# A DiT block on one core: scores in one block, attention in two halves, and transposes by DMA in place of TensorE

## The chip, the cores and the metric

The kernel runs on one core of a Trainium2 chip. The core has five engines that run side by side, each in the order of its own program: TensorE (PE, matrix multiplication into PSUM), VectorE (DVE), ScalarE (ACT), GpSimd (POOL) and SyncE (SP, which here only issues DMAs). The metric is the device time of one execution in microseconds (us), lower is better.

## The reference

One diffusion-transformer block with B = 2 batches of N = 256 tokens, D = 1152, two heads of width 576, and an MLP of width 4608, in bf16:

```
mod = (silu(c) @ w_mod).reshape(B, 6, 1, D)
shift_a, scale_a, gate_a, shift_m, scale_m, gate_m = [mod[:, i] for i in range(6)]
h = layernorm(x) * (1 + scale_a) + shift_a
q, k, v = split(h @ wqkv)                          # two heads of 576
attn = softmax(q @ k.T * 576 ** -0.5)              # per batch and head, 256 x 256
x = x + gate_a * ((attn @ v) @ wo)
h2 = layernorm(x) * (1 + scale_m) + shift_m
return x + gate_m * (gelu(h2 @ w_fc1) @ w_fc2)
```

## The kernel before

The 512 tokens are four tiles of 128 (`NT` = 4, two per batch). D is nine chunks of 128 (`KD` = 9), numbered 0 to 8. A head is 576 wide, which is four and a half chunks: chunk 4 (`HC`) holds 64 features of head 0 and 64 of head 1 (`HP` = 64). Sections that end in columns go in three panels of 384 (`PW`, `NPD` = 3).

The stages follow one another on PE: K projection with the first layer norm (to 33.5 us in the profile), Q projection (L454), attention scores and V projection interleaved (L482, L506), transposes of the attention weights (L546), attention times values (L567), output projection (`wo_group`, L634), FC1 (L681) and FC2 (L748).

Scores (`score_tile`, L473): one tile of 128 queries by 256 keys for each batch, head and query tile, eight in all, each ahead of one of the first eight V groups (a V group is one token tile by one panel, nine matmuls of 384 columns, L506). Each score tile has five matmuls. The chunk that both heads share is read from `kT4m`, a copy of K's chunk 4 in which the other head's 64 rows are zero. In the same way `v4m` is a zero-padded copy of V's chunk 4. The softmax of a tile is a maximum on DVE (L487), an exponential on ACT (L491), a reciprocal and a multiplication on DVE (L497, L498).

After V, PE transposes the attention weights in 16 blocks of 128x128 (L546), DVE and ACT copy them out of PSUM, and attention times values is made for both batches, chunk pair by chunk pair (L567), into `aT`.

The output projection runs over token tiles and panels, 12 groups (`wo_group`). After each, DVE multiplies by the gate (L640), POOL adds the residual (L641), and DVE gathers statistics (L646). When a tile is complete, `ln2_normalize` takes the root on ACT (L588), reciprocal and bias on DVE (L589, L591) and normalizes on ACT (L594), for the last tile with the tail of the row on DVE (L596). `ln2_transpose` then transposes the normalized chunks on PE (L605) into PSUM, and scales and shifts them on the way out, on ACT (L610) or DVE (L615), into `hT`. These transposes are dripped between matmuls by `filler`: those of batch 0 between the matmuls of the last three projection groups, those of batch 1 within FC1.

FC1 first runs ten of its 36 output chunks for batch 0 alone and then for batch 1 alone (`MSPLIT` = 10, 256-wide matmuls), and the other 26 for both (512-wide). `gate_m` comes from `dot_section` (L445): 18 products on DVE against `w_gate_mT`, a section of w_mod that the DMA engines transpose while loading it (L534). It then makes a round trip through DRAM (`gate_m_finish`). `gate_a` comes from a small section on PE (`gate_natural`, L414), is copied out by DVE and ACT (L422, L424), written to DRAM by POOL's DMAs (L425) and read back broadcast (L428). `shift_m` and `scale_m` are sections of 36 matmuls each (`vec_section`, L381); four matmuls at a time run in column quarters of the array.

Order is the program's order: at its end the kernel chains each engine's instructions in the order in which they were written (L762 to L772), SP among them. All big loads and DMA transposes are issued by SP. Five buffers of 20.7 KB a partition (the pool `wide`) hold all weights in turn, so a load also waits until the buffer's old content has been used. PSUM has six accumulators (`acc_tile`) and two smaller-use buffers (`aux_tile`). A new accumulator takes the buffer that was released first.

Of the kernel before, what the change touches and what calls it, by code (L numbers as in the profile page):

```python
# [19 lines left out]
def kernel(  # L20
# [88 lines left out]
    def load_section(name, s):  # L109
        w = wide_tile(name)  # L110
        for r in range(0, KD, 3):
            nc.sync.dma_start(w[:, r:r + 3, :], wmod_v[:, r:r + 3, s * D:(s + 1) * D])
        return w
# [9 lines left out]
    w_gate_a = load_section("w_gate_a", S_GATE_A)  # L123
    w_v = load_panels("w_v", wqkv_v, 2 * D)
    w_shift_m = load_section("w_shift_m", S_SHIFT_M)
    w_scale_m = load_section("w_scale_m", S_SCALE_M)
    w_o = load_panels("w_o", wo_v, 0)
    w_f1 = [None] * 4
    w_f1[0] = load_panels("w_f1_0", wfc1_v, 0)
    w_f1[1] = load_panels("w_f1_1", wfc1_v, D)  # L130
# [10 lines left out]
    kT4m = act.tile([P, H, T], BF16, name="kT4m")  # L141
    v4m = act.tile([P, NT, H, P], BF16, name="v4m")
    nc.gpsimd.memset(kT4m[HP:P, 0, :], 0.0)
    nc.gpsimd.memset(kT4m[0:HP, 1, :], 0.0)
    nc.gpsimd.memset(v4m[:, :, 0, HP:P], 0.0)
    nc.gpsimd.memset(v4m[:, :, 1, 0:HP], 0.0)

# [138 lines left out]
    def k_evac(m):  # L288
        if m == HC:
            evac(kT4m[0:HP, 0, :], pk[m][0:HP, :])  # L290
            evac(kT4m[HP:P, 1, :], pk[m][HP:P, :])
        else:
            evac(kT[:, m, :], pk[m][:])
# [157 lines left out]
    for m in range(KD):  # L451
# [7 lines left out]
        if m == 6:  # L459
            gate_a = gate_natural(0, w_gate_a)  # L460


    def head_chunks(h):
        return list(range(HC + 1)) if h == 0 else list(range(HC, KD))

    n_s = B * H * TPB
    soft = act.tile([P, 4 * n_s * N], BF16, name="soft", tag="x1")
    e_all = soft[:, 0:2 * n_s * N].bitcast(FP32).rearrange("p (i n) -> p i n", n=N)
    attn_all = soft[:, 2 * n_s * N:3 * n_s * N].rearrange("p (i n) -> p i n", n=N)
    attnT_all = soft[:, 3 * n_s * N:4 * n_s * N].rearrange("p (i c n) -> p i c n", c=TPB, n=N)  # L470
    attn_tiles = {}

    def score_tile(b, h, qt):  # L473
        chunks = head_chunks(h)
        q0 = b * N + qt * P
        ps_s = acc_tile([P, N], "ps_s")
        for i, cc in enumerate(chunks):
            if cc == HC:
                k_ap = kT4m[:, h, b * N:(b + 1) * N]
            else:  # L480
                k_ap = kT[:, cc, b * N:(b + 1) * N]
            nc.tensor.matmul(  # L482
                ps_s[:], qT[:, cc, q0:q0 + P], k_ap,
                start=(i == 0), stop=(i == len(chunks) - 1),
            )
        negmax = small.tile([P, 1], FP32, name="negmax", tag="negmax")
        nc.vector.reduce_max(negmax[:], ps_s[:], axis=AX.X, negate=True)  # L487
        si = (b * H + h) * TPB + qt
        e_sb = e_all[:, si, :]
        rowsum = small.tile([P, 1], FP32, name="rowsum", tag="rowsum")  # L490
        nc.scalar.activation(e_sb, ps_s[:], ACT.Exp, bias=negmax[:], scale=1.0, accum_out=rowsum[:])  # L491
        attn = attn_all[:, si, :]
        attn_tiles[(b, h, qt)] = attn

        def finish():
            rs = small.tile([P, 1], FP32, name="rs", tag="rs")
            nc.vector.reciprocal(rs[:], rowsum[:])  # L497
            nc.vector.tensor_scalar_mul(attn, e_sb, rs[:])  # L498

        return finish  # L500


    def v_group(pnl, t):
# [7 lines left out]
        c4 = HC * P - pnl * PW  # L511
        if 0 <= c4 and c4 + P <= PW:
            evac(v4m[:, t, 0, 0:HP], pacc[:, c4:c4 + HP])
            evac(v4m[:, t, 1, HP:P], pacc[:, c4 + HP:c4 + P])
# [4 lines left out]
    for i, (pnl, t) in enumerate(v_order):  # L519
        fin = score_tile(*score_order[i]) if i < len(score_order) else None  # L520
        v_group(pnl, t)
        if fin is not None:
            fin()
# [135 lines left out]
    while fill:  # L659
        fill.pop(0)()  # L660
# [142 lines left out]
```

## Time and profile before

| | us |
|---|---|
| median of 8 runs (lowest to highest) | 248.93 (248.54 to 249.13) |
| the profiled execution, its time | 248.76 |
| its span, first to last instruction | 247.0 |
| Q projection ends, scores begin | 52.29 |
| V ends, attention transposes begin | 76.85 |
| output projection begins | 82.28 |
| output projection ends, FC1 begins | 100.83 |
| FC2 begins | 173.13 |

The profiled execution's time is 1.76 us more than its span; the span is what the trace explains. The granted TensorE clock was 1.00 throughout. In the profile's rows a busy PE is modelled to the end of its pipeline, so the length of a piece overlaps the start of the next, and costs are best read from start to start. "Idle before" names how long an engine stood still before an instruction and what released it. Times in tables and timelines count from the start of the span. SP's rows ("SPq") are the issue of a DMA, not its transfer.

### The profile page before, as it was taken

The page shows a single profiled execution, that of the slowest core. Times are in us where ns is not written, and L with a number is a line of the kernel's source. Part 1 is how long each engine was busy: PE and PEld are TensorE (multiplying, and loading weights), DVE is VectorE, ACT ScalarE, POOL GpSimd, SP SyncE. Part 2 cuts the span into 40 slices and gives each one's busy share as a digit, 9 for nine tenths or more (in the row PEclk, how much of TensorE's full clock was granted, in tenths as well). Part 3 has the DMA queues.
Part 4 walks back from the last instruction along what each step waited for, and adds up shares of the span by engine and source line. Part 5 has one row for each costly group of instructions (what it writes and reads, how often), then busy time and mean ns, then how long its engine had stood idle before and what let it go on. Part 6 is the DMA issues. An engine that isn't in the chain of part 4 may idle for free.

```text
span 247.0 us, 4011 instructions
## 1 busy us (share of the span) xinstructions
PE 239.0 (97%) x1709; PEld 144.3 (58%) x1709; DVE 88.3 (36%) x209; ACT 68.3 (28%) x133; POOL 34.3 (14%) x53
## 2 busy tenths in 40 slices
PE   6899999999999999989999999999999999999994
PEld 2585444456657766878844444444666666666674
DVE  2752461335444678720099991000011000000001
ACT  6731341243424424593322233322000000000000
POOL 4000021031000266300000003100011122111111
PEclk9999999999999999999999999999999999999999
DMA  6999999999999999999792007999600000000000
GB/s 232 323 335 362 366 332 372 333 363 394 379 327 328 327 327 326 327 292 241 157 330 87 0 3 212 326 343 326 182 16 16 19 16 16 21 16 16 31 20 16
DMA packets 63837, 52.18 MB, mean 211 GB/s; under 512 B 12091, under 2 KB 58571, under 8 KB 63819
## 3 DMA queue, kind: packets, MB, share of 16 engines
q1 hardware_dynamic: 62928, 50.14, 66.9%
q0 software_dynamic: 864, 1.79, 2.1%
q8 instruction: 13, 0.21, 0.4%
q14 instruction: 5, 0.04, 0.0%
q10 hardware_dynamic: 27, 0.00, 0.0%
HBM read 48.08 MB, written 1.19 MB: 199 GB/s over the span
## 4 chain that ended last, share of the span: by engine, by line
PE 90%; DMA 3%; DVE 2%; ACT 2%; issue 1%; SPq 0%; ACTq 0%; DVEq 0%
PE pacc L748 28%; PE pacc L681 26%; PE pacc L506 7%; PE pacc L454 7%; PE pacc L634 7%; PE pk L265 4%; DMA w_scale_a<-in_w_mod_dram 3%; PE pk L298 2%; PE pa L567 2%; PE ps_s L482 2%; PE pn L381 1%; DVE stats L175 1%; PE pt L605 1%; PE pm L233 1%; PE pt L243 1%
## 5 line engine op out<-in xcount | busy, mean ns | idle before, releaser
L681 PE MATMUL pacc<-hT,w_f 128*128 128x512 bf16 (+1 forms) x414 | 71.1, 333 | 0.0
L748 PE MATMUL pacc<-w_f,gT 128*128 128x384 bf16 (+2 forms) x468 | 70.5, 314 | 0.0
L748 PEld LDWEIGHTS <-gT 128*128 128x128 bf16 x468 | 44.4, 98 | 26.3
L681 PEld LDWEIGHTS <-w_f 128*128 128x128 bf16 x414 | 40.3, 98 | 29.4
L754 DVE TENSOR_TENSOR tmp<-pacc,gate 128x384 f32<-128x384 f32 (+2 forms) x13 | 6.8, 527 | 88.0 <-PE pacc L748 88.0
L445 DVE SCALAR_TENSOR_TENSOR late<-w_gate_mT,late 128x1152 bf16<-128x1152 bf16 x18 | 24.4, 1358 | 12.4 <-DMA w_gate_mT<-in_w_mod_dram 11.9
L725 ACT ACTIVATE gT<-pacc 128x512 bf16<-128x512 f32 x26 | 15.5, 597 | 35.0 <-PE pacc L681 35.0
L756 POOL TENSOR_TENSOR o_sb<-tmp,x 128x384 bf16<-128x384 f32 (+1 forms) x12 | 11.7, 971 | 72.9 <-DVE tmp L754 72.9
L506 PE MATMUL pacc<-w_v,hT 128*128 128x384 bf16 x108 | 19.2, 326 | 0.0
L634 PE MATMUL pacc<-w_o,big 128*128 128x384 bf16 x108 | 18.5, 326 | 0.0
L454 PE MATMUL pacc<-hT,w_q 128*128 128x512 bf16 x81 | 17.8, 379 | 0.0
L641 POOL TENSOR_TENSOR x<-tmp,x_sb 128x384 f32<-128x384 f32 x11 | 10.0, 912 | 33.3 <-issue 27.2
L506 PEld LDWEIGHTS <-hT 128*128 128x128 bf16 x108 | 10.4, 98 | 6.3 <-issue 0.5
L634 PEld LDWEIGHTS <-big 128*128 128x128 bf16 x108 | 10.4, 98 | 6.2
L265 PE MATMUL pk<-big,w_k 128*128 128x256 bf16 (+2 forms) x90 | 13.4, 293 | 0.4 <-ACT big L252 0.4
L454 PEld LDWEIGHTS <-w_q 128*128 128x128 bf16 x81 | 7.9, 98 | 9.6 <-issue 0.3
L265 PEld LDWEIGHTS <-w_k 128*128 128x128 bf16 x90 | 7.5, 97 | 3.4 <-DMA w_k<-in_wqkv_dram 0.3
L436 POOL DMA_DIRECT2D gates_dram<-grow x4 | 2.0, 513 | 45.5 <-DVE grow L711 45.5
L284 DVE TENSOR_SCALAR big<-pacc 128x512 bf16<-128x512 f32 x5 | 3.5, 691 | 13.3 <-PE pacc L454 13.3
L640 DVE TENSOR_TENSOR tmp<-pacc,gate 128x384 f32<-128x384 f32 x12 | 6.7, 556 | 3.7 <-PE pacc L634 3.6
L697 ACT ACTIVATE gT<-pacc 128x512 bf16<-128x512 f32 x10 | 5.9, 598 | 7.4 <-PE pacc L681 7.4
L158 PE MATMUL pwarm<-zeros 128*128 128x512 bf16 x19 | 6.7, 501 | 1.2 <-DVE eps_t L92 1.2
(109 smaller groups left out, 171.3 us busy)
## 6 DMA issues: line engine op xcount, KB each, us to landing
w_f<-in_w_fc_dram SPq DMA_DIRECT2D x14, 864.0 KB, 10.2
w_f<-in_w_fc_dram SPq DMA_DIRECT2D x2, 2592.0 KB, 18.5
w_f<-in_w_fc_dram SPq DMA_DIRECT2D x2, 1728.0 KB, 13.3
w_shift_a<-in_w_mod_dram SPq DMA_DIRECT2D x3, 864.0 KB, 11.0
w_q<-in_wqkv_dram SPq DMA_DIRECT2D x3, 864.0 KB, 12.2
w_gate_a<-in_w_mod_dram SPq DMA_DIRECT2D x3, 864.0 KB, 10.1
w_v<-in_wqkv_dram SPq DMA_DIRECT2D x3, 864.0 KB, 12.7
w_shift_m<-in_w_mod_dram SPq DMA_DIRECT2D x3, 864.0 KB, 10.2
```

The lines of the kernel that those rows point to most:

```text
L158: nc.tensor.matmul(dst[:], zeros[:, 0:P], zeros[:], start=True, stop=True)
L265: nc.tensor.matmul(pk[m][:, c0:c1], w_k[:, k, m * P:(m + 1) * P], hT0[:, k, c0:c1], start=(k == 0 and c0 == 0), stop=(k == KD - 1), skip_g ...
L445: nc.vector.scalar_tensor_tensor(spill, wT[:, j, :], 1.0, s_all[:, b, :], op0=ALU.mult, op1=ALU.mult, accum_out=dst[:, b * KD + j:b * KD + ...
L454: nc.tensor.matmul(pacc[:], w_q[:, k, m * P:(m + 1) * P], hT[:, k, :], start=(k == 0), stop=(k == KD - 1),)
L506: nc.tensor.matmul(pacc[:], hT[:, k, t * P:(t + 1) * P], w_v[:, k, pnl * PW:(pnl + 1) * PW], start=(k == 0), stop=(k == KD - 1),)
L634: nc.tensor.matmul(pacc[:], aT[:, k, t * P:(t + 1) * P], w_o[:, k, c0:c1], start=(k == 0), stop=(k == KD - 1),)
L641: (nc.gpsimd if pool_add else nc.vector).tensor_tensor(x1[:, t, c0:c1], tmp[:], x_sb[:, t, c0:c1], op=ALU.add)
L681: nc.tensor.matmul(dst, w_f1[m // KD][:, k, ml * P:(ml + 1) * P], hT[:, k, c0:c1], start=(k == 0), stop=(k == KD - 1),)
L725: nc.scalar.activation(gT[:, m, :], pacc[:], ACT.Gelu_apprx_tanh)
L748: nc.tensor.matmul(pacc[:], gT[:, kk, t * P:(t + 1) * P], w_f2[j][:, r, c0 - n * PW:c0 - n * PW + cw], start=(kk == 0), stop=(kk == KF - 1),)
L754: nc.vector.tensor_tensor(tmp[:], pacc[:], gate_m[:, b, c0:c0 + cw], op=ALU.mult)
L756: (nc.vector if last else nc.gpsimd).tensor_tensor(o_sb[:], tmp[:], x1[:, t, c0:c0 + cw], op=ALU.add)
```

## The change

- Scores are made in one block ahead of V: for each batch and head one accumulator of 128 x 2 x 256 is filled by four full chunks, then the shared chunk 4 is added by matmuls over 64 rows only, at row position 0 for head 0 and 64 for head 1. `kT4m` and `v4m`, their memsets and their evictions are gone.
- The softmax is made per batch and head (`softmax`): one maximum over both query tiles, two exponentials, one reciprocal, two multiplications. The first two stand ahead of V group 0, the third ahead of group 1, the fourth ahead of group 2.
- The attention weights of a batch are transposed by one DMA from SBUF to SBUF (`attn_transpose`, issued by SP) in place of eight PE transposes and their copies.
- The gate section moves from the Q stage to after V group 1.
- Attention times values and the first half of the output projection are made for batch 0, then attention times values for batch 1, then the `shift_m` and `scale_m` sections (which stood in V), then the second half of the projection. The shared chunk is made for both batches at once from 64-column matmuls (`pv_shared`).
- After the layer norm of a token tile one DMA transposes it from SBUF into `hT` (`ln2_transpose`), and `ln2_modulate` scales and shifts `hT` in place, two of three chunks on DVE, the third on ACT: batch 0 after projection group (3,0), batch 1 after the last matmuls of FC1's batch-0 part. The `filler` is gone.
- `MSPLIT` is 8 in place of 10.
- Loads on SP stand in another order: w_v ahead of w_gate_a; w_o and w_shift_m ahead of the attention transposes; w_scale_m and w_f1_0 behind them; w_f1_1, w_f1_2, w_f1_3 and w_gate_mT behind the last LN2 transpose.
- The residual addition of the last panel of tiles 1 and 3 is DVE's, all others POOL's (before: of tile 3 alone).

```diff
-    w_gate_a = load_section("w_gate_a", S_GATE_A)
+    w_gate_a = wide_tile("w_gate_a")
     w_v = load_panels("w_v", wqkv_v, 2 * D)
+    load_section("w_gate_a", S_GATE_A, w_gate_a)
+    w_o = load_panels("w_o", wo_v, 0)
     w_shift_m = load_section("w_shift_m", S_SHIFT_M)
-    w_scale_m = load_section("w_scale_m", S_SCALE_M)
-    w_o = load_panels("w_o", wo_v, 0)
-    w_f1 = [None] * 4
-    w_f1[0] = load_panels("w_f1_0", wfc1_v, 0)
-    w_f1[1] = load_panels("w_f1_1", wfc1_v, D)
...
+    scores = {}
+    for b in range(B):
+        for h in range(H):
+            scores[b, h] = acc_tile([P, TPB, N], "ps_s")
+            for qt in range(TPB):
+                q0 = b * N + qt * P
+                for i in range(HC):
+                    cc = h * (HC + 1) + i
+                    nc.tensor.matmul(
+                        scores[b, h][:, qt, :], qT[:, cc, q0:q0 + P], kT[:, cc, b * N:(b + 1) * N],
+                        start=(qt == 0 and i == 0), stop=False, skip_group_check=True,
+                    )
+    for b in range(B):
+        for qt in range(TPB):
+            q0 = b * N + qt * P
+            for h in range(H):
+                rows = slice(h * HP, (h + 1) * HP)
+                nc.tensor.matmul(
+                    scores[b, h][:, qt, :], qT[rows, HC, q0:q0 + P], kT[rows, HC, b * N:(b + 1) * N],
+                    start=False, stop=True, skip_group_check=True, tile_position=(h * HP, 0),
+                )
+
+    def softmax(b, h):
+        ps_s = scores[b, h]
+        negmax = small.tile([P, TPB], FP32, name="negmax", tag="negmax")
         nc.vector.reduce_max(negmax[:], ps_s[:], axis=AX.X, negate=True)
+        rowsum = small.tile([P, TPB], FP32, name="rowsum", tag="rowsum")
+        s0 = (b * H + h) * TPB
+        for qt in range(TPB):
+            nc.scalar.activation(
+                e_all[:, s0 + qt, :], ps_s[:, qt, :], ACT.Exp, bias=negmax[:, qt:qt + 1], scale=1.0,
+                accum_out=rowsum[:, qt:qt + 1],
+            )
+        rs = small.tile([P, TPB], FP32, name="rs", tag="rs")
+        nc.vector.reciprocal(rs[:], rowsum[:])
+        for qt in range(TPB):
+            nc.vector.tensor_scalar_mul(attn_all[:, s0 + qt, :], e_all[:, s0 + qt, :], rs[:, qt:qt + 1])
+
+    def attn_transpose(b):
+        n_b = H * TPB
+        nc.sync.dma_start_transpose(
+            attnT_all[:, b, :, :],
+            attn_all[:, b * n_b:(b + 1) * n_b, :].rearrange("p i n -> p (i n)"),
+        )
...
     for i, (pnl, t) in enumerate(v_order):
-        fin = score_tile(*score_order[i]) if i < len(score_order) else None
+        for j in ((0, 1), (2,), (3,))[i] if i < 3 else ():
+            softmax(j // H, j % H)
+            if j % H == H - 1:
+                attn_transpose(j // H)
         v_group(pnl, t)
+        if i == 1:
+            gate_a = gate_natural(0, w_gate_a)
+
+    w_scale_m = load_section("w_scale_m", S_SCALE_M)
+    w_f1 = [None] * 4
+    w_f1[0] = load_panels("w_f1_0", wfc1_v, 0)
...
+    def pv_shared():
+        pa = acc_tile([P, B, TPB, P], "pa")
+        for b in range(B):
+            for kc in range(TPB):
+                for h in range(H):
+                    f0 = HC * P + h * HP
                     nc.tensor.matmul(
+                        pa[h * HP:(h + 1) * HP, b, :, :], v_sb[:, b * TPB + kc, f0:f0 + HP], attnT(b, h, kc),
+                        start=(b == 0 and kc == 0), stop=(kc == TPB - 1),
+                        skip_group_check=True, tile_position=(0, h * HP),
                     )
+        evac(aT[:, HC, :], pa[:].rearrange("p b q n -> p (b q n)"))
+
+    pv_chunks(0, 0)
+    pv_chunks(0, 1)
+    pv_shared()
...
+    def ln2_transpose(t):
+        nc.sync.dma_start_transpose(hT[:, :, t * P:(t + 1) * P], xn2[t][:])
+
+    def ln2_modulate(b):
+        for k in range(KD):
+            h = hT[:, k, b * N:(b + 1) * N]
+            if k % 3 == 2:
                 nc.scalar.activation(
+                    h, h, ACT.Identity, bias=shift_m[:, k, b:b + 1], scale=scale_m[:, k, b:b + 1],
                 )
             else:
                 nc.vector.tensor_scalar(
+                    h, h, scale_m[:, k, b:b + 1], shift_m[:, k, b:b + 1], op0=ALU.mult, op1=ALU.add,
                 )
...
     for o, (t, i) in enumerate(order):
-        if (t, i) == (3, 0):
-            fill_ln2(0, 5)
-        wo_group(t, i, o < len(order) - 1)
-        if o:
+        wo_group(t, i)
+        if o and (t, i) != (TPB, 0):
             ln2_stats(*order[o - 1])
-    while fill:
-        fill.pop(0)()
-    ln2_normalize(NT - 2, False)
+        if (t, i) == (TPB - 1, NPD - 1):
+            ln2_stats(t, i)
+            pv_chunks(1, 0)
+            pv_chunks(1, 1)
+            shift_m = vec_section(sT, w_shift_m, "shift_m")
+            scale_m = vec_section(sT, w_scale_m, "scale_m")
+            nc.vector.tensor_scalar_add(scale_m[:, :, 0:B], scale_m[:, :, 0:B], 1.0)
+        if (t, i) == (NT - 1, 0):
+            ln2_modulate(0)
     ln2_stats(*order[-1])
+
+    w_f1[1] = load_panels("w_f1_1", wfc1_v, D)
+    w_f1[2] = load_panels("w_f1_2", wfc1_v, 2 * D)
+    w_f1[3] = load_panels("w_f1_3", wfc1_v, 3 * D)
+    w_gate_mT = wide_tile("w_gate_mT")
...
-    MSPLIT = 10
+    MSPLIT = 8
...
+            if b == 0 and m0 == MSPLIT - 2:
+                ln2_modulate(1)
             nc.scalar.activation(gT[:, m0:m0 + 2, b * N:(b + 1) * N], pacc[:], ACT.Gelu_apprx_tanh)
```

## The prediction, as it was made before the result was known

> **What bounds the kernel now.** I read the busy shares first, then the slices, then TensorE's timeline over the stage that changes, and last the DMA queue's own issues.
>
> From the page's busy list and slices:
>
> ```profile
> PE 239.0 (97%) x1709; PEld 144.3 (58%) x1709; DVE 88.3 (36%) x209; ACT 68.3 (28%) x133; POOL 34.3 (14%) x53
> ...
> PE   6899999999999999989999999999999999999994
> ...
> DMA  6999999999999999999792007999600000000000
> ```
>
> TensorE (PE) is busy from slice 2 to the end, so a microsecond counts only if it leaves PE's order of work or is put into it. The DMA engines are nearly full up to about 123 us: a transfer put in there stands behind others.
>
> PE's timeline (start, length, line, operation, count, idle before it):
>
> ```profile
> 48.40 4.06 PE L454 MATMUL pacc<-hT,w_q 128*128 128x512 bf16 x18
> ...
> 76.85 1.06 PE L546 MATMUL pTt<-ident,soft 128*128 128x128 bf16 x16
> 77.91 1.03 PE L567 MATMUL pa<-soft,big 128*128 128x256 bf16 x8
> ...
> 96.25 0.39 PE L605 MATMUL pt<-ident,xn 128*128 128x128 bf16 x4
> 96.47 0.98 PE L634 MATMUL pacc<-w_o,big 128*128 128x384 bf16 x5
> ...
> 100.83 5.40 PE L681 MATMUL pacc<-hT,w_f 128*128 128x256 bf16 x48
> ...
> 109.41 0.38 PE L605 MATMUL pt<-ident,xn 128*128 128x128 bf16 x4 [0.98 <-ACT hT L610]
> 109.63 1.04 PE L681 MATMUL pacc<-hT,w_f 128*128 128x256 bf16 x8
> ```
>
> Lengths overlap the next piece by PE's pipeline, so I take costs from start to start: a 128x128 transpose 0.055 us (76.85 to 77.91 is 16 of them; 96.25 to 96.47 is 4), a 256-wide matmul 0.109 (5.24 for 48), a 384-wide one 0.163 (0.81 for 5), a 512-wide one 0.217. The output-projection stage ends at 100.83, FC2 begins at 173.13. The only wait of this stage is the 0.98 us.
>
> SP's queue and who waited for the last of its transposes:
>
> ```profile
> 101.87 9.81 SPq L534 DMA_TRANSPOSE w_gate_mT<-in_w_mod_dram  x1
> 111.73 3.85 SPq L534 DMA_TRANSPOSE w_gate_mT<-in_w_mod_dram  x1
> 115.62 4.09 SPq L534 DMA_TRANSPOSE w_gate_mT<-in_w_mod_dram  x1
> 123.51 1.36 DVE L445 SCALAR_TENSOR_TENSOR late<-w_gate_mT,late 128x1152 bf16<-128x1152 bf16 x1 [11.86 <-DMA w_gate_mT<-in_w_mod_dram]
> ```
>
> These are the trace's only DMA transposes: 27 blocks of 128x128 each. Issuing takes 3.85 to 4.09 us (the first, 9.81, stood behind loads), and the last landed at 123.4, 7.8 us after its issue began.
>
> **The change, part by part.**
>
> *PE work that goes.* 16 attention transposes: 0.89. 36 LN2 transposes: 36 x 0.055 = 1.98. The 0.98 us wait for a transposed PSUM tile goes with its tile. FC1 with the split at 8 in place of 10 costs the same (two 256-wide matmuls 0.218, one 512-wide 0.217). The gate section (1.21, from 47.19 to 48.40) moves from the Q stage into the V stage: nothing on PE. PE sum: -3.85. The four memsets on POOL and the split evictions into kT4m and v4m also go: worth nothing, as the memsets end at 3.2 us, while PE's first real work waits for w_scale_a until 8.8, and the evictions lie under V's matmuls.
>
> *Half-height and half-width matmuls.* The chunk shared by both heads took 8 zero-padded matmuls in the scores and 8 in attention times values, 0.87 each. Now each 8 are half-array ones, in neighbouring pairs that can run together. Nearest row: the four-way packed section at 74.16 takes 1.22 us to its end at 75.38 for 9 slots of four 288-wide matmuls, 1.08 of streaming (288/256 x 0.109 x 9 is 1.10) and some 0.14 extra. So 4 slots x 0.109 + 0.14 = 0.58 each: -0.29 twice, -0.6. Ends: no pairing, 0; pairing free of extras, -0.87. The Trainium skill's page "TensorEngine Tiling (Array Packing)", "Key Properties", says that changing the tiling mode drains the array; the 0.14 is what the row shows of that, and I use it.
>
> *Softmax in one go per batch and head.* The reduction now spans 512 PSUM columns: 0.42 us at 256, plus 0.27 (copies L282 take 0.425 at 256 columns and 0.692 at 512), 0.68. Then two exponentials with accumulator reads (1.02), reciprocal, two multiplications, some 2.6 us for each of four, in series, since VectorE (DVE) waits for ScalarE (ACT) inside each. Q ends at 52.29 - 1.21 = 51.1, scores (32 x 0.109 + 0.58) at 55.15. The first two are done at about 60.2. Behind them on DVE: V's first eviction, the third softmax, the gate's copies, the fourth, done at 66.8. V's fifth group takes the buffer of V's first (evicted at 60.7, wanted at 62.2), the sixth that of the third softmax (62.4 against 63.7), the eighth that of the fourth (65.9 against 66.6). So no wait on PE, by as little as 0.7. The gate's copies start at 63.2 rather than 48.5; from copy to landed gate the old trace takes some 15 us (copies 48.49, second broadcast issued 56.9, landing 6 to 8 later), giving 78.2, and its first reader is due at about 78.2. A late gate delays DVE, and PE has six accumulators ahead of it: nothing.
>
> *Attention transposes on SP.* Issued at 60.3 and 66.9, behind the loads through w_shift_m; what SP has behind them is w_scale_m and w_f1_0, wanted at 88 and 98. Before, the 28th load was issued at 53.27 and landed some 15 us later, at 68 to 69. The two transposes (8 blocks each, 1.2 us at 4.09/27 a block) land behind it at 70 to 72. V ends at 55.15 + 12 x 1.465 + 1.21 = 73.9: hidden, by 2 to 4 us. Without that cover it would be PE time one for one.
>
> *Values of batch 0, projection, batch 1.* 16 x 0.109 + 0.58: to 76.3. The projection reads chunk 4 after four matmuls (0.65), but that is the one evicted last (0.2 latency + 0.69): PE waits 0.3 to 0.7, I take 0.5. Six groups of 9 x 0.163 to 85.6; values of batch 1 1.74; two sections 2.43, moved here from V; six groups: projection ends at 98.5, against 100.83.
>
> *LN2 of batch 0.* Tile 1 follows the old last tile's chain (100.83 to 106.05, less 0.8 for work of another tile in it): normalized at 90.0, transposed by 94. DVE comes to the modulation only after tile 2's statistics, at 97.75: six operations at 0.20 (L402's row: 12 in 2.44). ACT comes to its three only after normalizing tile 2 (1.35, L594). Projection group (3,0) ends at 95.6; with the old spacing tmp to ACT's normalize 2.16, ACT is free at 99.3, and chunk 2 is ready at 99.7, wanted at 98.7. Chunks 5 and 8 follow 0.42 apart. FC1 loses 1.2 us, and its first half runs 72 x 0.109 = 7.85, to 107.6.
>
> *LN2 of batch 1, the term that decides.* After 98.5 DVE still has tmp(3,1), its statistics, tmp(3,2), the addition, two statistics (0.5 each), aggregation, root, reciprocal, bias; ACT's 640 columns end at 104.2. The transpose: 9 blocks from SBUF, with SP and the DMA engines idle. By the row: issue 9/27 x 4 = 1.35, then the tail after issue (123.4 - 119.7 = 3.7, partly its own backlog, so 1.5 to 3.7): 3 to 5, I take 4.0. A rule speaks against it: "VectorE: DVE Perf Modes", "The three transpose paths", gives 1309 ns for one 128x128 block by the DMA crossbar. Nine in a row would be 11.8 us. The row's 27 blocks in 4.1 (0.15 each) say that they overlap, so I follow the row; by the rule the kernel would end 7.8 us later, at 254.7. No trace here shows an SBUF source, which is why it stays in the range. With 4.0: landed 108.2, chunks modulated from 108.6, wanted from 107.6. PE loses 1.1 in all.
>
> *FC1's remaining weights.* w_f1_1 to w_f1_3 now stand on SP behind that last transpose: issued from 105.6, 2.63 us per load. w_f1_1 is wanted at 108.7 + 7.85 + 1.95 = 118.5 and lands by 115; w_f1_2 lands by 123 (wanted 136). The gate's transposed weights follow at 129 and land between 142 and 151; their 25 us of dot products and 16 us of round trip end between 184 and 192. The first reader, at 177, waits, yet PE needs that accumulator only after six groups, at 206. The last w_f2 load waits for those dot products (by 176, landing by 195), wanted at 219. Nothing.
>
> *Sum.* -3.85 - 0.6 + 0.5 + 1.2 + 1.1 = -1.65. Walking the clock gives a little more: 107.6 + 1.1 + 7.85 + 252 x 0.2165 = 171.1 for FC2's start against 173.13, -2.0 (the sum's 0.35 is slack between stages; I keep the clock). Against the profiled 248.76 (span 247.0): 246.8; the shown runs' median, 248.93, gives 246.9. I predict 246.9.
>
> **Rivals.** *No new waits show* (transposes land in 3 us, ACT's queue slips through): -3.85 - 0.6 is 244.5, less up to 0.35 of the slack above: 244.3. For it: both FC1 waits are computed to about 1 us. Against: ACT's order is fixed by the program.
>
> *The batch-1 transpose is slow.* Every microsecond over 4.0 lands on PE. At 6.0 the change is worth nothing; at 8, 250.9; at 11.8, 254.7. For it: an SBUF source is untried here and the crossbar rule. Against: SP and the engines are idle then.
>
> *The attention transposes land after V.* They sit behind a backlog of 8 us and must pass it; from 76 on (2 us late) the gain is gone, at 78 it is 250.9. For it: the first w_gate_mT issue took 9.81 behind loads. Against: 2 to 4 us of cover.
>
> *Halves don't pair up:* +0.6, 247.5, the same side.
>
> **How the numbers follow.** As forecast, 245.6 to 248.2: 0.52. No waits, 243.9 to 245.6: 0.13. A break-even mixture around 248.2 to 249.4: 0.12. Slow batch-1 transpose 0.15 and late attention transposes 0.08, 249.4 to 255. About 0.2% (0.5 us) is what a measurement tells from no change. Faster 0.65, same 0.10, slower 0.25. Leaving out 1 in 10 at the fast end and 1 in 10 at the slow end: 244.8 to 250.8; the likeliest case alone is 245.6 to 248.2.
>
> **What would show it.** Right: FC2's first matmul near 171; no PE transposes after the K stage; waits of about a microsecond each before FC1's first group (on ACT) and before batch 1's first group (on the transpose); the two attention transposes landed by 72. Wrong: a batch-1 transpose of over 6 us from issue to landing, PE idle before attention times values, PE waiting on w_f1_1, or V groups waiting for softmax.

## The result and the profile after

The changed kernel takes 247.85 us (median of 11 runs, 247.28 to 248.65) against 248.92 us (median of 32, 248.54 to 249.68) for the kernel before: 0.9956 of the time, 95% interval 0.9948 to 0.9965, a gain of 1.07 us. The forecast was 246.9, so the sign was right and the gain about half of the one computed. The profiled execution took 247.42 us with a span of 245.6, against 248.76 and 247.0. The granted TensorE clock is 1.00 in both. In the experiments below, an execution that took over 1.5% longer than the fastest of its kernel (one each in two experiments) is left out of the median and the ratio.

First the busy list and the slices of the page after:

```profile
PE 237.0 (97%) x1639; PEld 138.7 (56%) x1639; DVE 86.1 (35%) x200; ACT 63.1 (26%) x122; POOL 31.8 (13%) x48
...
PE   6899999999999989899999999999999999999994
...
DMA  6999999999999990399999999996960000000000
```

PE still fills the span. With slices of 6.14 us, its two eights in the middle stand at 86 to 92 and at 98 to 104 us, where before there was one, at 105 to 111. From 92 to 104 us the DMA engines have almost nothing to do (a 0 and a 3), where they were loading weights before.

Then PE's timeline over the changed stages (start, length, line, operation, count, and in brackets the idle time before it and what ended it):

```profile
50.97 3.66 PE L458 MATMUL ps_s<-big 128*128 128x256 bf16 x32
54.55 0.61 PE L467 MATMUL ps_s<-big 64*128 64x256 bf16 x8
...
73.97 1.91 PE L530 MATMUL pa<-attnT_all,big 128*128 128x256 bf16 x16
75.81 0.63 PE L542 MATMUL pa<-attnT_all,big 128*64 128x256 bf16 x8
76.37 9.16 PE L597 MATMUL pacc<-w_o,big 128*128 128x384 bf16 x54
85.36 1.91 PE L530 MATMUL pa<-attnT_all,big 128*128 128x256 bf16 x16
...
90.22 8.95 PE L597 MATMUL pacc<-w_o,big 128*128 128x384 bf16 x54 [0.64 <-ACT big L265]
99.01 0.38 PE L657 MATMUL pacc<-hT,w_f 128*128 128x256 bf16 x2
100.34 8.13 PE L657 MATMUL pacc<-hT,w_f 128*128 128x256 bf16 x70 [0.95 <-ACT hT L582]
108.80 21.49 PE L657 MATMUL pacc<-hT,w_f 128*128 128x256 bf16 x132 [0.33 <-DVE hT L586]
...
171.56 8.61 PE L721 MATMUL pacc<-w_f,gT 128*128 128x384 bf16 x52
```

FC2 begins at 171.56 instead of 173.13: 1.57 us gained by then, of which the span keeps 1.4. The two pauses that were forecast are there. FC1 starts at 99.01, and its third matmul comes at 100.34 (about 1.1 lost). Batch 0's last four matmuls begin at 107.87, so at 0.109 us each its work ends at 108.31, and batch 1's part starts at 108.80: a pause of 0.5. Within batch 0's part another 0.34 is lost behind the third matmul (66 matmuls from 100.34 to 107.87 take 7.53 us, where 66 x 0.109 is 7.19), as ScalarE's chunks come one by one; the 0.8 that the experiments below speak of are these two together. A third pause was not in the working: 0.64 us at 90.22, waiting for an eviction of attention times values on ACT.

SP's queue, from the attention transposes on (the issue, not the transfer):

```profile
60.10 8.24 SPq L490 DMA_TRANSPOSE attnT_all<-soft  x2
...
86.17 20.14 SPq L574 DMA_TRANSPOSE hT<-xn  x4
106.36 20.60 SPq L118 DMA_DIRECT2D w_f<-in_w_fc_dram  x9
```

The attention transposes start at 60.1, as soon as the first softmaxes are done. FC1's remaining weights come behind the last LN2 transpose.

Last, the end of the chain that ended last (start, length, work), between the projection and batch 1's first matmul:

```profile
90.22 6.04 PE pacc L597 x36
96.29 0.56 DVE tmp L602
...
98.28 1.62 DVE hT L586 x6
...
103.94 0.93 ACT xn L566
104.89 3.41 DMA hT<-xn
...
108.80 62.93 PE pacc L657 x324
```

The chain leaves PE at 96.29 and comes back at 108.80. In between it is DVE's work on tiles 2 and 3 with batch 0's modulation, one normalization on ACT and one transpose. The pause ahead of FC1 isn't in it: PE lost 1.1 us there, but had it not, it would have stood longer in front of batch 1. The third experiment tests that.

### The profile page after: what moved, and what is told of

It is laid out like the page before. It is cut to its first block, busy times and chain, and to the rows that moved or that the text cites. A ratio compares the mean times of both kernels' runs of the same rounds, so it can differ in the third digit from the quotient of the medians.

```text
span 245.6 us, 3868 instructions
## 1 busy us (share of the span) xinstructions
PE 237.0 (97%) x1639; PEld 138.7 (56%) x1639; DVE 86.1 (35%) x200; ACT 63.1 (26%) x122; POOL 31.8 (13%) x48
## 4 chain that ended last, share of the span: by engine, by line
PE 85%; DVE 6%; DMA 4%; ACT 2%; issue 1%; SPq 0%; DVEq 0%; ACTq 0%
PE pacc L721 29%; PE pacc L657 26%; PE pacc L503 7%; PE pacc L438 7%; PE pacc L597 5%; PE pk L253 4%; DMA w_scale_a<-in_w_mod_dram 3%; PE pk L282 2%; DVE stats L608 2%; PE ps_s L458 1%; DMA hT<-xn 1%; DVE tmp L602 1%; DVE hT L586 1%; ACT xn L566 1%; DVE stats L163 1%; PE pa L530 1%
## 5 line engine op out<-in xcount | busy, mean ns | idle before, releaser
L657 PEld LDWEIGHTS <-w_f 128*128 128x128 bf16 x396 | 38.7, 98 | 33.8 <-issue 2.5
L698 ACT ACTIVATE gT<-pacc 128x512 bf16<-128x512 f32 x28 | 16.7, 597 | 37.7 <-PE pacc L657 37.7
L503 PE MATMUL pacc<-w_v,hT 128*128 128x384 bf16 x108 | 17.9, 326 | 0.0
L603 POOL TENSOR_TENSOR x<-tmp,x_sb 128x384 f32<-128x384 f32 x10 | 9.1, 910 | 20.2 <-DVE tmp L602 13.3
L146 PE MATMUL pwarm<-zeros 128*128 128x512 bf16 x19 | 7.2, 532 | 1.2 <-DVE eps_t L92 1.2
L420 POOL DMA_DIRECT2D s_dram<-s_rows x4 | 2.6, 654 | 34.3 <-DVE s_rows L423 34.3
L240 ACT ACTIVATE big<-pt,scale_a 128x256 bf16<-128x256 bf16 (+1 forms) x12 | 4.6, 434 | 8.9 <-PE pt L231 7.4
```

What stands on the lines that cost most here:

```text
L146: nc.tensor.matmul(dst[:], zeros[:, 0:P], zeros[:], start=True, stop=True)
L503: nc.tensor.matmul(pacc[:], hT[:, k, t * P:(t + 1) * P], w_v[:, k, pnl * PW:(pnl + 1) * PW], start=(k == 0), stop=(k == KD - 1),)
L603: (nc.gpsimd if i < NPD - 1 or t % TPB == 0 else nc.vector).tensor_tensor(x1[:, t, c0:c1], tmp[:], x_sb[:, t, c0:c1], op=ALU.add)
L657: nc.tensor.matmul(dst, w_f1[m // KD][:, k, ml * P:(ml + 1) * P], hT[:, k, c0:c1], start=(k == 0), stop=(k == KD - 1),)
L698: nc.scalar.activation(gT[:, m, :], pacc[:], ACT.Gelu_apprx_tanh)
```

## The experiments

All times are medians, and each ratio is against runs of the kernel before on the same chip. "After" is the changed kernel, whose 247.85 us come from its own comparison; the kernel before took 248.86 to 248.96 in those of the experiments and 248.92 there, so a difference from after of 0.1 us says nothing.

### Nine modulations moved ahead

```diff
         wo_group(t, i)
+        if (t, i) == (NT - 1, 0):
+            ln2_modulate(0)
         if o and (t, i) != (TPB, 0):
             ln2_stats(*order[o - 1])
...
-        if (t, i) == (NT - 1, 0):
-            ln2_modulate(0)
```

> Edit to the changed kernel: batch 0's modulation is put ahead of the statistics and the normalization of token tile 2, so that ACT does its three chunks before the 1.35 us normalization. Theory A (one chain: DVE's work after projection group (3,0), then the transpose of tile 3 and its modulation, sets when FC1's batch-1 part may begin; TensorE's pause before FC1 has slack behind it): the 1.1 us pause of TensorE at FC1's beginning (99.2 to 100.3 us) goes, the pause before batch 1's part grows from 0.8 to some 1.9, and the time stays within 0.3 us of the changed kernel's 247.85. Theory B (every pause of TensorE costs its own length): 1.1 us faster, 246.7.

Measured: 250.2 us, 1.0049 of before (1.0032 to 1.0067). Neither theory: 2.35 us more than after. PE's timeline of this kernel, and below it two stretches (width, then for PE, weight loads, DVE, ACT and POOL the busy time and the number of instructions, then the granted clock, the DMA share and GB/s):

```profile
110.24 19.95 PE L657 MATMUL pacc<-hT,w_f 128*128 128x256 bf16 x118 [3.04 <-DVE hT L586]
```

```profile
107.00:111.00 4.00, 0.96 (x6) 0.48 (x5) 1.16 (x5) 2.69 (x6) 0.00 (x0) 1.00 0.96 221
111.00:115.00 4.00, 4.00 (x23) 2.87 (x22) 0.47 (x2) 1.49 (x3) 0.00 (x0) 0.57 1.09 339
```

The pause ahead of FC1 is gone (it begins at 99.18), as both theories said, but batch 1 starts at 110.24, 1.44 later than in after, and then PE runs at a mean granted clock of 0.57 for 4 us, which is 1.7 us lost. Within them the clock is halved for 3.4 us, and full again behind that:

```profile
111.10:114.50 3.40, 3.40 (x17) 2.35 (x17) 0.37 (x2) 1.17 (x3) 0.00 (x0) 0.50 1.08 340
114.50:118.00 3.50, 3.50 (x34) 3.13 (x32) 0.00 (x0) 0.82 (x2) 0.00 (x0) 1.00 1.10 327
```

Of the 1.44, 0.16 was there before the edit could matter (values of batch 1 begin at 85.52 instead of 85.36). Some 0.6 come from DVE (its timeline in this kernel; the same group in after stands in the chain above, at 98.28):

```profile
96.93 2.21 DVE L586 TENSOR_SCALAR hT<-hT,scale_m,shift_m 128x256 bf16<-128x256 bf16 x6
```

The six modulations take 2.21 us instead of 1.62; the longest of them took 0.939 us instead of 0.34, in a stretch in which an addition ran on POOL (97.09 to 98.03); in after no addition ran beside them. The Trainium skill, page "SBUF — State Buffer", "SBUF: two separate sides", tells of a port pair that GpSimd and some VectorE operations lock against each other for a whole instruction. That fits this one row, but no run here separates it. So the last transpose is issued 0.8 later. It also takes 4.09 us instead of 3.41, the remaining 0.68; whether the edit has to do with that isn't shown.

### The pause filled with matmuls

The kernel just described, with matmuls on zeros between the halves of FC1's single-batch part. Their result is not read.

```diff
+        if b == 0:
+            warm(12, acc_tile([P, T], "pfill"))
```

> The kernel with all nine modulations of batch 0 moved ahead (250.2 us, a pause of 3.04 us ahead of batch 1, and a granted clock of 0.57 in 111 to 115 us), with twelve more matmuls of 512 columns on zeros in the pause, whose result nobody reads (about 2.6 us of the 3.04). Theory A (the pause makes the chip grant TensorE a lower clock behind it, and that costs 1.7 us: 4 us at 0.57): the clock stays at 1.00 in 111 to 115 us and the time falls to 248.3 to 248.8. Rival B (the added time is DVE's and the transposes' alone): 250 to 250.5, no change.

Measured: 248.83 us, 0.9995 of before (0.9985 to 1.0005), 1.4 us less than without the filling and 0.03 above theory A's band. The granted clock stays at 1.00:

```profile
111.00:115.00 4.00, 4.00 (x36) 3.29 (x34) 0.60 (x3) 1.62 (x4) 0.00 (x0) 1.00 1.10 327
```

Batch 1 starts at 110.38, no earlier than before the filling, and FC2 at 173.14: 62.76 us later, to the hundredth what after needs (108.80 to 171.56). Without the filling it was 64.25 (110.24 to 174.49). So PE's standing still costs a second time, by the clock that it is granted afterwards. The Trainium skill, page "TensorE: Matmul & The Clock Gate", "What's actually happening", has the clock halved after an idle window of about 3.4 us. The pause of the first experiment was near that (3.04); the next experiment shows that a much shorter one can do it too.

### Only ScalarE's three modulations moved ahead

```diff
         wo_group(t, i)
+        if (t, i) == (NT - 1, 0):
+            ln2_modulate(0, "a")
...
         if (t, i) == (NT - 1, 0):
-            ln2_modulate(0)
+            ln2_modulate(0, "d")
```

> The changed kernel with ScalarE's three modulations of batch 0 put ahead of its normalization of tile 2; DVE's six stay where they are. Theory A (the start of batch 1's half is set by the chain of DVE work and the DMA transpose of tile 3, which does not move): FC1 begins without its pause, batch 1 waits about 1.9 us instead of 0.8 and starts at the same 108.8, and the time is within 0.25 of 247.85. Rival B (the pauses add up): 1.0 us less, 246.7 to 246.9. Unlike the order that moved all nine modulations, no pause reaches 3 us, so the granted clock stays at 1.00 in 111 to 115 us, where that order showed 0.57.

Measured: 249.0 us, 0.9997 of before (0.9975 to 1.002), 1.15 more than after. The mechanism of theory A is there: FC1 without its pause (72 matmuls in one piece from 98.83), and batch 1 at 108.78, no earlier than after's 108.80:

```profile
108.78 21.45 PE L661 MATMUL pacc<-hT,w_f 128*128 128x256 bf16 x123 [1.75 <-DVE hT L588]
```

```profile
107.00:111.00 4.00, 2.25 (x13) 1.47 (x13) 1.63 (x6) 2.64 (x6) 0.00 (x0) 0.82 0.92 245
111.00:115.00 4.00, 4.00 (x29) 3.20 (x28) 0.00 (x0) 0.70 (x2) 0.00 (x0) 0.75 1.10 335
```

But the clock falls after a pause of only 1.75 us. The 0.82 and 0.75 are means over stretches that cut the fall in two. It is the same one as in the first experiment, 3.4 us at half clock:

```profile
106.00:109.60 3.60, 1.85 (x15) 1.20 (x13) 1.22 (x5) 2.81 (x6) 0.00 (x0) 1.00 0.92 184
109.60:113.00 3.40, 3.40 (x17) 2.34 (x17) 0.40 (x2) 1.10 (x3) 0.00 (x0) 0.50 1.09 344
113.00:115.00 2.00, 2.00 (x20) 1.79 (x19) 0.00 (x0) 0.42 (x2) 0.00 (x0) 1.00 1.10 331
```

FC2 comes 64.24 us after batch 1's start (173.02) in place of 62.76. This part of the expectation was wrong. The twelve executions split by their mean granted clock: four with 0.997 to 1.0 took 247.45 to 247.74 us, eight with 0.990 to 0.993 took 248.87 to 249.98. So theory A holds for the work, and by its mechanism the pauses do not add up; the loss against after is the clock's. A pause alone doesn't decide it: the 2.03 us of the next experiment were followed by a clock of 1.00. Nor does the fall come at a fixed time: here it begins 2.5 us after PE's last work (107.03 to 109.6), in the first experiment 3.9 (107.20 to 111.1). What decides it is open.

### Attention weights transposed on TensorE again

```diff
-        nc.sync.dma_start_transpose(
-            attnT_all[:, b, :, :],
-            attn_all[:, b * n_b:(b + 1) * n_b, :].rearrange("p i n -> p (i n)"),
-        )
+        for h in range(H):
+            pTt = acc_tile([P, TPB, TPB, P], "pTt", BF16)
+            for qt in range(TPB):
+                for kc in range(TPB):
+                    nc.tensor.transpose(
+                        pTt[:, qt, kc, :], attn_all[:, b * n_b + h * TPB + qt, kc * P:(kc + 1) * P], ident[:],
+                    )
+            evac(...)
...
+    attn_transpose(0)
+    attn_transpose(1)
     pv_chunks(0, 0)
```

> The changed kernel with the attention weights transposed on TensorE again, behind the last group of values, instead of by DMA. Theory A (what TensorE saves on the way to the output projection is on the path that sets the end, since the chain of DVE work and DMA behind it starts from TensorE's groups): the 16 transposes take 1.06 us from start to start as in the trace of before (76.85 to 77.91), the evictions behind them add up to 0.3, so 248.8 to 249.2 us against 247.85. Rival B (the end is set by something that does not move with TensorE): within 0.3 of 247.85.

Measured: 249.0 us, 1.0006 of before (0.9984 to 1.0028), with a wide spread of 247.79 to 250.81. The median is in theory A's band, but in part by something else. In the timeline the transposes are back between V and attention times values, from 74.07 to 74.98, which is 0.91 us. The projection begins at 77.37, 3.30 us after V's end in place of 2.40:

```profile
74.07 1.06 PE L494 MATMUL pTt<-ident,soft 128*128 128x128 bf16 x16
74.98 1.91 PE L535 MATMUL pa<-attnT_all,big 128*128 128x256 bf16 x16
...
111.52 18.68 PE L664 MATMUL pacc<-hT,w_f 128*128 128x256 bf16 x118 [2.03 <-DVE hT L593]
```

Batch 1's start is 2.7 later rather than 1.0, because in this execution the DMA transpose of tile 3 took 5.11 us in the chain, not 3.41. The four fastest, 247.79 to 248.21, would fit a short one, but no trace of them shows it. Whether this edit itself makes a long one more frequent isn't shown.

### LN2's transposes on TensorE again

```diff
-    def ln2_transpose(t):
-        nc.sync.dma_start_transpose(hT[:, :, t * P:(t + 1) * P], xn2[t][:])
+    def ln2_transpose(b, ks, eng):
+        pt = aux_tile([P, len(ks), N], "pt", BF16)
...
+                    filler()
...
-    MSPLIT = 8
+    MSPLIT = 10
```

> The changed kernel with LN2's transposes on TensorE again, as before the change (36 transposes between the matmuls, modulation out of PSUM, ten output chunks by single batch); all the rest of the change stays. Theory A (the DMA transposes save 2.0 us of TensorE and give as much back: 1.1 to 1.2 us ahead of FC1, 0.8 ahead of batch 1 and 0.3 in its first group): 247.4 to 248.2 us, no more than 0.4 from the changed kernel's 247.85. Rival B (the gain of the change comes from these transposes): 249 us or more.

Measured: 247.96 us, 0.9962 of before (0.9950 to 0.9974). This is theory A: within 0.11 of after, so in the median LN2's DMA transposes, the largest part of the computed gain, are worth nothing that these runs can tell. The two profiled executions lie further apart, 248.13 and 247.42; this one is the slowest of its five, after's is one of its fastest. With them on PE there is no pause ahead of FC1 (it begins at 100.28), one of 0.98 us at 108.86 as in the kernel before, and the same 0.64 ahead of the second half of the projection.

### Tile 3's transpose issued twice

```diff
-        nc.sync.dma_start_transpose(hT[:, :, t * P:(t + 1) * P], xn2[t][:])
+        for _ in range(2 if t == NT - 1 else 1):
+            nc.sync.dma_start_transpose(hT[:, :, t * P:(t + 1) * P], xn2[t][:])
```

> Edit to the changed kernel: the DMA transpose of token tile 3 is issued twice, the second waiting for the first (the output is the same). Theory A: each transpose takes 3.4 us from issue to landing and lies on the chain whole, so the time grows by 3.4 to 4.0 us, to 251.3 to 251.9. Rival C (FC1's batch-0 part covers the transpose with room to spare, and the 0.8 us pause has another cause): under 1 us more.

Measured: 251.87 us, 1.0124 of before (1.0098 to 1.0150), so the time of theory A, but by two causes. Batch 1's start moves by 2.89, from 108.80 to 111.69. Counted from V's end, which is 0.30 earlier here, it is 3.19, and the two transposes in the chain, 3.25 and 3.34 in place of one of 3.41, make 3.18. Behind it the clock falls as in the first experiment:

```profile
111.69 18.68 PE L658 MATMUL pacc<-hT,w_f 128*128 128x256 bf16 x113 [3.52 <-DVE hT L587]
```

```profile
112.00:116.00 4.00, 4.00 (x22) 2.89 (x22) 0.92 (x4) 1.68 (x4) 0.00 (x0) 0.57 1.08 340
```

From 112.0 to 115.4 the clock is 0.50. FC2 comes 64.06 after that start (175.75), 1.3 more than in after. The transpose is on the path one for one; the price of each further microsecond is more than one once the pause is long.

### Nine output chunks by single batch

```diff
-    MSPLIT = 8
+    MSPLIT = 9
```

> Edit to the changed kernel: FC1's part by single batches takes nine output chunks in place of eight, which puts 0.98 us more of batch 0 in front of batch 1's part; the total of matmul work is the same (2 x 0.109 against 0.217 us per pair). Theory A: the pause before batch 1's part (0.8 us, with another 0.3 of waits chunk by chunk inside its first group) shrinks by 0.8 to 1.0, and the time with it, to 246.9 to 247.1. Rival C: no change, since the pause has another cause.

Measured: 247.13 us, 0.9926 of before (0.9906 to 0.9945), as theory A has it. Behind the wait at its third matmul, FC1's timeline shows no further pause, and batch 1's first group follows batch 0's last at once. Some 0.65 is still lost in short waits for single chunks (FC2 begins at 171.40, 70.70 after this line; 160 x 0.109 + 243 x 0.2165 is 70.05):

```profile
100.70 29.64 PE L657 MATMUL pacc<-hT,w_f 128*128 128x256 bf16 x212 [0.95 <-ACT hT L582]
```

### Tile 1's normalization behind batch 1's attention times values

```diff
         if (t, i) == (TPB - 1, NPD - 1):
-            ln2_stats(t, i)
             pv_chunks(1, 0)
             pv_chunks(1, 1)
+            ln2_stats(t, i)
```

> Edit to the changed kernel: the statistics and the normalization of token tile 1 are put behind batch 1's attention times values, so that ACT and DVE evict those accumulators before they normalize. Theory A with the step that the prediction left out (these evictions stand behind tile 1's normalization, 0.92 us on ACT, and TensorE waits 0.64 us for them before projection group (2,0)): the pause goes and everything behind it moves up, 0.6 to 0.8 us faster, 247.05 to 247.25. Rival D: the later normalization of tile 1 delays its transpose and batch 0's modulation, and the gain is given back: within 0.2 us of the changed kernel.

Measured: 246.93 us, 0.9913 of before (0.9894 to 0.9931), 0.92 less than after and a little more than theory A had (0.6 to 0.8). ScalarE's timeline shows it, first this kernel, then after:

```profile
87.22 0.58 ACT L265 CAST big<-pa 128x512 bf16<-128x512 f32 x1 [0.25 <-PE pa L530]
...
90.33 0.92 ACT L566 ACTIVATE xn<-x,nb,rstd 128x640 bf16<-128x640 f32 x1 [0.54 <-DVE nb L563]
```

```profile
88.78 0.92 ACT L566 ACTIVATE xn<-x,nb,rstd 128x640 bf16<-128x640 f32 x1 [0.54 <-DVE nb L563]
89.61 1.05 ACT L265 CAST big<-pa 128x512 bf16<-128x512 f32 x2
```

The evictions no longer stand behind the normalization, and PE's second half of the projection starts without a wait:

```profile
89.87 8.95 PE L597 MATMUL pacc<-w_o,big 128*128 128x384 bf16 x54
...
108.73 26.45 PE L657 MATMUL pacc<-hT,w_f 128*128 128x256 bf16 x155 [0.61 <-DVE hT L586]
```

In this profiled execution, the slowest of five, FC1 begins 24.34 us after V's end (74.31) in place of 25.04, so 0.70 is won, and FC2 97.18 after it in place of 97.59: 0.41. The rest went into the pause ahead of batch 1, whose chain moved up by 0.41 only; that much of rival D is right. How the median comes to 0.92 isn't seen in one trace, and its interval reaches 0.5 us to either side.

### The last two together

> The two single changes that were measured alone, put together: tile 1's normalization behind batch 1's attention times values (0.92 us less, alone) and nine output chunks by single batch (0.72 less, alone). If they add up (A): 246.1 to 246.4 us. If both only took away the same pause ahead of batch 1 (B): 246.8 to 247.0.

Measured: 246.22 us (246.07 to 246.73), 0.9896 of before (0.9880 to 0.9911). They add up, as in A: 247.85 - 0.92 - 0.72 is 246.21. That it fits to a hundredth is luck, with intervals of 0.4 us to either side, but B's 246.8 to 247.0 lies above all five runs. It is the fastest of all versions here, 2.7 us below the kernel before and 1.6 below after. The one pause that the timeline still shows between V and FC2 is the 0.95 ahead of FC1's third matmul:

```profile
99.59 30.71 PE L657 MATMUL pacc<-hT,w_f 128*128 128x256 bf16 x215 [0.95 <-ACT hT L582]
...
170.29 9.91 PE L722 MATMUL pacc<-w_f,gT 128*128 128x384 bf16 x60
```

### Ten chunks, weights asked for early, with and without ScalarE's move

```diff
     w_f1[0] = load_panels("w_f1_0", wfc1_v, 0)
+    w_f1[1] = load_panels("w_f1_1", wfc1_v, D)
...
-    MSPLIT = 8
+    MSPLIT = 10
```

Both kernels have this and the reordered evictions. The first also has ScalarE's three modulations of batch 0 ahead.

> All that the runs so far point to, in one: tile 1's statistics and normalization behind batch 1's attention times values, ScalarE's three modulations of batch 0 ahead of its normalization of tile 2, ten output chunks by single batch instead of eight, and the second part of FC1's weights asked for ahead of LN2's transposes, since chunk 9 needs it. Theory A (the time is TensorE's work and its pauses; each pause that is removed counts once enough of batch 0's work covers the chain behind tile 3): from the 246.93 of the reordered evictions, less the pause of 0.95 ahead of FC1, 0.61 ahead of batch 1 and some 0.2 in its first group: 245.0 to 245.6 us, FC1 from its first matmul to FC2 without a pause. Rival B (the end is set by the chain of DVE work and DMA, and ScalarE's order adds nothing, as it did alone): 246 to 246.5.

> The same without the move of ScalarE's three modulations. Theory A: the pause of 0.95 ahead of FC1 is back and now counts in full, since ten chunks leave no pause ahead of batch 1 to take it in: 0.9 to 1.1 us above the run with the move, 246.0 to 246.5. Rival B: the same time as with the move, within 0.2.

Measured: 250.5 us with ScalarE's move, 1.0065 of before (1.0044 to 1.0086), and 248.03 without it, 0.9958 of before (0.9936 to 0.9981), spread from 246.83 to 249.26. Both theories of both runs were wrong, by something that neither had looked at. The DMA queue on SP in the kernel with the move:

```profile
70.28 20.00 SPq L118 DMA_DIRECT2D w_f<-in_w_fc_dram  x6
90.38 19.25 SPq L575 DMA_TRANSPOSE hT<-xn  x4
```

The three loads put ahead keep SP until 90.28, so the first LN2 transpose is issued at 90.38 instead of 86.17, with issues of up to 5.2 us and up to 8.1 us to landing behind those loads. Batch 0's `hT` then lands only at 99.5. With ScalarE's move, ACT waits for it (8.79 us), and tile 2's root (at 101.14) and normalization stand behind:

```profile
99.65 1.58 ACT L585 ACTIVATE hT<-hT,shift_m,scale_m 128x256 bf16<-128x256 bf16 x3 [8.79 <-DMA hT<-xn]
```

FC1 starts at 102.17, after a pause of 3.73 us and with a clock of 0.79 from 99 to 107 us (0.50 from 101.9 to 105.3); without the move it is 100.08 and 1.73, and a pause of 1.30 us stands ahead of batch 1 (111.89) besides, behind a last transpose of 5.09 us. What ScalarE's move is worth once no pause follows it could not be seen this way, and stays open.

### The halves of the shared chunk apart

```diff
-    for b in range(B):
-        for qt in range(TPB):
-            q0 = b * N + qt * P
-            for h in range(H):
+    for h in range(H):
+        for b in range(B):
+            for qt in range(TPB):
+                q0 = b * N + qt * P
```

(and the same in `pv_shared`)

> The changed kernel with the matmuls of the shared chunk in an order by head, so that the two halves of TensorE no longer take turns (eight in the scores, eight in attention times values). Theory A (two such matmuls run at once only where they stand next to each other): each row of eight takes 0.87 us (0.109 each, as one of 256 columns in the trace of before) instead of 0.55, 0.64 more in all, so 248.4 to 248.6 us. Rival B (halves of the tile run at this speed in any order): within 0.2 of 247.85.

Measured: 248.01 us, 0.9962 of before (0.9950 to 0.9974). Rival B: the eight matmuls of the scores take 0.55 us from start to start, those of attention times values 0.57 (76.16 to 76.73), as in pairs. PE's timeline over the first:

```profile
54.90 0.62 PE L467 MATMUL ps_s<-big 64*128 64x256 bf16 x8
55.45 3.10 PE L503 MATMUL pacc<-w_v,hT 128*128 128x384 bf16 x18
```

The price used in the forecast was right. So is its picture of halves that run at the same time, except that partners needn't be neighbours in the program. The records of single matmuls show it: here two of the eight have begun by 54.91 us, four by 55.03, six by 55.14 and eight by 55.25, so they come in pairs about 0.11 us apart, as in after (54.56, 54.68, 54.79, 54.90). That such a pair has one matmul of each head is inferred, and what brings partners together that the kernel lists apart isn't shown.

## Why the prediction was right, and its gain nearly twice too large

- *PE work that goes.* Right. The attention transposes are worth what was put down: 0.89 computed, 0.91 on PE's clock when they are put back (1.15 in the median, in which longer last transposes have a part). The half-array matmuls: 0.58 computed, 0.55 and 0.56 measured.
- *Softmax, gate and attention transposes hidden under V.* Right. V begins at 55.10 (computed 55.15) and attention times values at 73.97 (73.9), and no V group waits. The two transposes take 9.8 and 4.0 us from issue to landing and land at 69.9 and 70.6, ahead of V's end by over 3 us; the forecast had 70 to 72.
- *The wait for the chunk that is evicted last.* Too large: 0.5 was taken, some 0.1 shows behind the fourth matmul of the projection.
- *The missed term.* The step "Six groups of 9 x 0.163 to 85.6; values of batch 1 1.74; two sections 2.43" went straight on to the last six groups and asked nothing of ACT. On it, the evictions of batch 1's attention times values stand behind tile 1's normalization in program order, the same kind of order that the forecast did find in the pause ahead of FC1. PE waits 0.64. Reordered, that wait is gone and the median falls by 0.92.
- *LN2 of batch 0.* Near: 1.2 forecast; 1.1 ahead of the third matmul and 0.34 behind it make 1.45.
- *LN2 of batch 1.* Right in kind, near in size. The transpose was put at 4.0; those whose landing the trace shows take 3.4 to 5.0, and tile 3's 3.4 in the profiled execution. PE was to lose 1.1 in all. The pause is 0.5, but batch 1's first group then runs slower than computed, by some 0.36: FC2 follows batch 1's start by 62.76 us, where 7.85 + 252 x 0.2165 is 62.4. The chunks come at the pace of the modulation, which was costed by a row with one scalar operand (0.20 us each on DVE, 0.42 on ACT). With two it takes some 0.26 (1.62 for six) and 0.49 (1.57 for three, less the last one's tail). The Trainium skill's page "VectorE: DVE Perf Modes", "The three transpose paths", has 1309 ns for one block by DMA. Nine times that, the estimate of 11.8 us, is not what these transposes of nine blocks show: they land after 3.4 to 5.0.
- *The remaining weights.* Right: they are issued from 106.36 (computed 105.6), and neither FC1 nor FC2 waits for one.

In sum: FC2 was computed at 171.1 and begins at 171.56. By stages the 0.46 are +0.69 where the evictions were missed (85.36 to 90.22 is 4.86, computed 4.17), +0.36 in batch 1's first group, -0.31 for the chunk that is evicted last (76.37 to 85.36 is 8.99, computed 9.3), -0.41 in FC1's first half and the pause behind it, and +0.13 in the rest. So the nearness is in part luck: errors of 1.18 us late and 0.72 early. The prediction's plain sum, -1.65, comes nearer still to the measured -1.57, and by more luck, since it has the 0.64 at nothing and 0.5 for the chunk where 0.1 shows. The span keeps 1.4 us and the profiled time 1.34. The median of 11 runs shows 1.07, since the profiled execution is one of the faster ones. The length of the last transpose varies from one execution to the next (3.41 us in after's chain, 5.11 in that of another kernel) and lies on the path, which moves the median away from any one profile. That is argued, not shown run by run.

Where the computed gain went can be read from start to start against the kernel before, with work that only moved set off. In the profiled executions the attention transposes give 0.91, the half-array matmuls 0.62 and the time ahead of the scores 0.11. LN2's transposes give 0.74: 1.98 of PE work and the 0.98 us wait go, and 2.22 of waiting in FC1 come. The evictions take 0.59 and the projection 0.22. That is the 1.57. With LN2's transposes back on TensorE the profiled execution is 0.71 slower, which agrees, but the median only 0.11. So in the median hardly anything is left of the 2.96 that the change takes out there: it comes back as waiting for a chain that ends in a transpose of changing length.

## What to carry to other kernels

Work that leaves the busiest engine counts only as far as the chain that replaces it is covered. Here 36 transposes of 0.055 us were traded for a DMA of 3.4 us with its waits, and in these runs it was more work put in front of it (nine chunks instead of eight, 0.72 us) that made the trade pay. When a stage is moved, list on every engine and queue what the moved instructions now stand behind: the evictions behind a normalization on ACT cost 0.64 us of PE's time, and transposes behind weights on SP turned an expected 246.0 to 246.5 us into 248. And a reorder that removes one pause can lengthen another one downstream: follow the chain to the end before counting the gain.

## What the hardware showed that was not expected

- After some pauses of PE the granted clock is halved for 3.4 us, then full again. Four traces show it, after pauses of 1.75, 3.04, 3.52 and 3.73 us; in longer stretches it appears as 0.57, or as 0.82 and 0.75. Three of them show the cost between batch 1's start and FC2, 1.3 to 1.5 us (64.06 to 64.25 us against 62.76), and filling the pause of 3.04 us with idle matmuls brings it back to 62.76. It isn't certain for a given pause: by their mean clock eight of twelve executions of one kernel had it, four had not, and a pause of 2.03 us in another kernel was followed by a clock of 1.00.
- Eight matmuls of 256 columns over half the array, listed head by head, take as long as in alternation: 0.55 us, where one after the other they would take 0.87. In both orders they begin in pairs about 0.11 us apart; what pairs them when they are listed apart isn't shown.
- One modulation on DVE, in bf16 and in place, took 0.94 us instead of 0.34 in a stretch in which POOL ran an addition of 0.94 us. One case, not tested further.
